# Edge messages on one core: the buckets' one-hot rows are made on ScalarE instead of VectorE

## The chip, the cores and the metric

The kernel runs on one core of one Trainium2 chip. The metric is the device time of one execution of the whole program in microseconds (us); the kernel before was timed in three runs and its median counts. One further execution was taken by the hardware profiler, and every row of a profile below is from such an execution.

The core's engines are named as in the profile: PE is the matmul engine (PEld its weight loads), DVE is VectorE, ACT is ScalarE, POOL is GpSimd, and SP is SyncE, which issues most of the transfers. Each engine runs its own instructions in the order in which they were written, and they wait for each other by semaphores. ACT and DVE have no way round an instruction that waits: what is written behind it waits as well.

## The reference

One layer of message passing on a graph of N = 12,500 nodes with 64 values each and E = 800,000 edges with 16 values each:

```
m_in = concatenate([x[src], x[dst], e_attr], axis=-1)
msg  = silu(m_in @ w_msg)                 # one row of 64 for each edge
agg  = segment_sum(msg, dst, N)           # summed by the edge's target
out  = silu(concatenate([x, agg], axis=-1) @ w_upd)
```

The targets `dst` come in no order, so the kernel sorts the edges into buckets of targets before it sums them.

## The kernel before

**Buckets and chunks.** The nodes are cut into 128 buckets of 98. The edges are read in chunks of M = 8 tiles of 128 edges, 782 chunks in all. `seg_prep` computes for each edge, 18 chunks at once, the bucket `hi` of its target (`floor_ops`) and the target's place `lo` in the bucket. A chunk then goes through five steps, each a method of `Chunk`:

- `onehot` (L362) writes `hf`, a row of 128 for each edge, which is 1 at the edge's bucket and 0 elsewhere: one DVE comparison over 8 x 128 = 1024 elements a partition.
- `sums` (L368 to L371) adds these rows over the tiles of each half of the chunk: the first piece is copied on ACT, the other three are DVE additions, into `G`.
- `count` (L379 to L381) multiplies `hf` and `G` on PE, which leaves in `z` the place of each edge among the edges of its bucket; `ranks` (L386) takes it out on DVE.
- `expand` (L395 to L399) lays the edges' records into slots `X` on DVE; `move` (L407) brings them to their buckets' rows by 16 PE instructions with `hf` as weights, and ACT copies the result to `blk` (L409); `place` (L415, L416) advances the buckets' pointers on DVE.
- `scatter` (L420) writes `blk` to the buckets' places in a store in HBM, by an indirect transfer that POOL issues.

**Groups and batches.** Whole tiles of sorted edges are taken from the store in groups of up to 64 tiles (`fourth`, `middle` and `fifth` choose them with small DVE operations and two small PE products, L511 and L518, which use the same PSUM buffer as `move`). A group is worked on in batches of 8 tiles: `gather` (L574) fetches the sources' rows by eight indirect transfers of POOL; `onehot` of the batch (L579, L580) makes rows `q` for the targets within the bucket; `transpose` (L588 on PE, copied by ACT at L591 into `qt`); `product` (L597, PE); `message` (L603 on DVE, then SiLU at L604 on ACT); `parts` (L612, two DVE subtractions that split the message into bf16 parts); `reduce` (L623, PE) and `add` (L636 and L638, DVE). The first groups take single tiles and pairs of tiles of a bucket; later ones take four tiles of a bucket at a time, and only these have `parts`.

**A period.** The function `period` interleaves one step of each of several chunks and batches, and its text is the order of every engine's instructions. In one call there are: the chunk `h` that begins, the chunk `z` that is one period old, the chunk `p` that is two periods old and `s` that is three; and the batches `q`, `t` and `a` of ages 0, 1 and 2. So what `onehot` and `sums` make in one period is used by `count` in the next, by `move` in the one after, and the buffer of `hf`, of which there are three, is written again after that. In each period, after the message of batch `a`, DVE does `hf`, `parts`, `G`, `q`, `rank`, `X`, the sums and the pointers; ACT does SiLU, two copies of weights, `qt`, the first piece of `G`, a part of `q`, `blk`, and in one period of three the records (L257). There are 782 periods with a chunk; behind them come periods with batches alone and the updates of the nodes.

Of the kernel before, what the change touches and what calls it, by code (L numbers as in the profile page):

```python
# [6 lines left out]
AF = mybir.ActivationFunctionType  # L7
OP = mybir.AluOpType
# [6 lines left out]
P = 128  # L15
NBK = 128
BK = 98
# [5 lines left out]
M = 8  # L23
# [20 lines left out]
def mpnn_kernel(tc, x, e_attr, src, dst, w_msg, w_upd, out):  # L44
    nc = tc.nc
# [21 lines left out]
    with es:  # L67
# [21 lines left out]
        iof = cp.tile([P, P], F32, name="iof")  # L89
# [22 lines left out]
        ioB = cb[:, 0:P]  # L112
# [107 lines left out]
        T1, GAP = NT - NT % M, -NT % M  # L220
# [11 lines left out]
        def seg_load(load, n):  # L232
            di = sg.tile([P, SEG], I32, name="sdi")
            si = sg.tile([P, SEG], I32, name="ssi")
            load(di[:, :n], dst_v)
            load(si[:, :n], src_v)
            return di, si

        def seg_prep(di, si, n, t0=0):
            hi = sg.tile([P, SEG], F32, name="shi")  # L240
            lo = sg.tile([P, SEG], F32, name="slo")
            floor_ops(hi[:, :n], lo[:, :n], di[:, :n], HI_SC, HI_OFF)
            nc.vector.scalar_tensor_tensor(out=lo[:, :n], in0=hi[:, :n], scalar=-float(BK), in1=di[:, :n], op0=OP.mult, op1=OP.add)
            k = max(0, T1 - t0)
            if k < n and GAP:

                nc.vector.memset(hi[:, k:T1 + GAP - t0], float(2 * P))
            return hi, lo, si

        def ea_load(load, n):  # L250
            ea = eap.tile([P, EAT, DE], F32, name="ea")
            load(ea[:, :n, :], ea_v)
            return ea

        def records(ea, si, lo, n):
            rec = eap.tile([P, EAT, R], F32, name="rec")
            nc.scalar.activation(rec[:, :n, 0:DE], ea[:, :n, :], AF.Copy)  # L257
            nc.vector.scalar_tensor_tensor(out=rec[:, :n, DE], in0=lo, scalar=1.0 / 256, in1=si, op0=OP.mult, op1=OP.add)
            return rec
# [10 lines left out]
        def prep_seg(i):  # L270
            if i < len(segs) and i not in ready:
                load_seg(i)
                ready[i] = seg_prep(*loaded[i], segs[i][1], segs[i][0])
# [80 lines left out]
        class Chunk:  # L354
# [4 lines left out]

            def onehot(c):  # L360
                c.hf = hp.tile([P, M, NBK], F32, name="hf")
                nc.vector.tensor_tensor(out=c.hf, in0=ioB[:, None, :].to_broadcast([P, M, NBK]), in1=c.hi[:, :, None].to_broadcast([P, M, NBK]), op=OP.is_equal)  # L362

            def sums(c):

# [277 lines left out]
        def period(chunk=None, batch=None, ptr_new=None):  # L643

            h, z, p, s = chunk, pipe["h"], pipe["z"], pipe["p"]
            q, t, a = batch, pipe["q"], pipe["t"]
            forms = [g for g in work["forming"] if not g.ready()]
            pipe.update(h=h, z=z, p=p, q=q, t=t)
            if z:
                z.count()  # L650
            if a:
                a.message()
            if t:
                t.transpose(0)
            if h:
                h.onehot()
            if t:
                t.weights()
                t.transpose(1)
            if q:  # L660
                q.gather(0, BT // 2)
            if s:
                s.scatter()
            if q:
                q.gather(BT // 2, BT)
            if a:
                a.parts()
            if h:
                h.sums()
            if q:  # L670
                q.onehot()
            if z:
                z.ranks()
            for g in forms:
                g.fourth()
            if z:
                z.expand()
            if p:
                p.move()
            if a:  # L680
                a.reduce()
                a.add()
            if p:
                p.place(ptr_new)
            for g in forms:
                g.middle()
                g.fifth()
            if t:
                t.product()
            return a  # L690
# [141 lines left out]
        while pipe["p"]:  # L832
            period(None, take())
# [11 lines left out]
        for k in range(0, NCH, 512):  # L845
            n = min(512, NCH - k)
# [124 lines left out]
        with tc.If(more > 0):  # L971
# [4 lines left out]
            with tc.If(nover > 0):  # L976
# [12 lines left out]
                for k in range(0, NCH, P):  # L989
                    n = min(P, NCH - k)  # L990
# [12 lines left out]
                with tc.For_i(0, nover, 1):  # L1003

                    nc.vector.tensor_reduce(out=f1[:, 3:4], in_=fl, axis=AX.X, op=OP.min)
                    nc.vector.scalar_tensor_tensor(out=fl, in0=fl, scalar=f1[:, 3:4], in1=fl, op0=OP.not_equal, op1=OP.mult)
                    nc.vector.tensor_scalar(out=f1[:, 2:3], in0=f1[:, 3:4], scalar1=BIG, scalar2=None, op0=OP.add)

                    w0 = cp.tile([1, 2], F32, name="w0")
                    nc.vector.tensor_scalar(out=w0[:, 0:1], in0=f1[:, 2:3], scalar1=float(M), scalar2=float(NT - M), op0=OP.mult, op1=OP.min)  # L1010
                    nc.vector.scalar_tensor_tensor(out=w0[:, 1:2], in0=f1[:, 2:3], scalar=float(M), in1=w0[:, 0:1], op0=OP.mult, op1=OP.subtract)
                    nc.vector.tensor_copy(fi[:, 2:3], w0[:, 0:1])
                    bps = pp.tile([P, 512], F32, name="bps", tag="pl")
                    nc.tensor.matmul(bps[:, 0:1], oner, w0[:, 1:2], start=True, stop=True)
                    skip = cp.tile([P, 1], F32, name="skip")
                    nc.vector.tensor_copy(skip, bps[:, 0:1])
                    tv = nc.values_load(fi[0:1, 2:3], engines=(ENG.SP,), min_val=0, max_val=NT - M, skip_runtime_bounds_check_because="the start of a chunk")
                    window = lambda buf, src: nc.sync.dma_start(buf, src[:, ds(tv, M)])
                    hi, lo, si = seg_prep(*seg_load(window, M), M, -NT)
                    rec = records(ea_load(window, M), si[:, :M], lo[:, :M], M)  # L1020
                    off = cp.tile([P, M], F32, name="off")
                    nc.vector.tensor_scalar(out=off, in0=iof[:, 0:M], scalar1=skip, scalar2=float(2 * P), op0=OP.is_lt, op1=OP.mult)
                    nc.vector.tensor_tensor(out=hi[:, :M], in0=hi[:, :M], in1=off, op=OP.add)
                    c = Chunk(hi[:, :M], rec[:, :M, :])
                    c.onehot()
                    c.sums()
                    c.count()
                    c.ranks()

                    c.expand()  # L1030
                    c.move()
                    left = cp.tile([NBK, 3], F32, name="left")
                    nc.vector.tensor_scalar(out=left[:, 1:2], in0=c.blk[:, 1:2], scalar1=0.0, scalar2=None, op0=OP.is_gt)
                    nc.vector.tensor_tensor(out=left[:, 0:1], in0=c.blk[:, 0:1], in1=left[:, 1:2], op=OP.mult)
                    nc.vector.memset(rs, 0.0)
# [39 lines left out]
```

## Time and profile before

| | |
|---|---|
| median of 3 runs | 11522.06 us (11520.64 to 11545.6) |
| the profiled execution, its own time | 11522.43 us |
| its span, from the first instruction to the last | 11520.6 us |
| mean granted clock of PE | 0.817 |
| first and last `hf` (L362) | 13.9 and 10592.5 us |

In the rows that follow, a row of a group gives line, engine, operation, what is written and read, shapes and count; behind the first bar the busy time in us and the mean duration of one in ns; behind the second the idle time of the engine just before these instructions, and what ended it. A row of the timeline gives the start and the duration in us, then engine, line and operation, and in square brackets the idle time before it. A releaser that is called "remote" or "another core or an unknown queue" is a semaphore update for which the profile finds no instruction that ended at that moment. On one core that is no other core.

### The profile page before, as it was taken

How to read it: one execution, taken by the hardware profiler on the slowest of the kernel's cores; microseconds unless marked ns; L12 is line 12 of the kernel's file. 1: busy time of each engine (PE TensorE's matmuls, PEld its weight loads, DVE VectorE, ACT ScalarE, POOL GpSimd, SP SyncE). 2: the span in 40 equal slices, each digit the busy share in tenths (PEclk: the TensorE clock that was granted, in tenths of full speed). 3: DMA queues.
4: the chain of work that ended last, by engine and by line, in shares of the span. 5: the costliest groups of instructions: out<-in, count | busy, mean ns of one | idle time of the engine just before them, and what ended most of it. 6: DMA issues, size and time to landing. Idle time of an engine off the chain costs nothing. (4 is left out here: it accounts for less than half of the span.)

```text
span 11520.6 us, 142616 instructions
## 1 busy us (share of the span) xinstructions
PE 8812.3 (76%) x43298; PEld 6708.3 (58%) x44060; DVE 8786.3 (76%) x18300; ACT 2487.4 (22%) x5785; POOL 6874.6 (60%) x7129
## 2 busy tenths in 40 slices
PE   7777777777777777777777777777777777777566
PEld 4555555555555555655655555565655565555466
DVE  8777777888888888878888888887888888887322
ACT  2111112222222222222222222222222222222111
POOL 2455556666666666666666666666666666666555
PEclk9888888888888888788888888888888888888555
DMA  2111111111111111111111111111111111111212
GB/s 64 39 43 46 41 44 49 44 47 46 44 47 44 48 43 47 47 44 47 44 47 44 46 47 44 47 44 47 47 43 47 45 46 47 43 46 41 44 36 39
DMA packets 661675, 521.39 MB, mean 45 GB/s; under 512 B 472583, under 2 KB 520135, under 8 KB 660903
## 3 DMA queue, kind: packets, MB, share of 16 engines
q0 software_dynamic: 252672, 378.89, 12.3%
q1 hardware_dynamic: 405527, 132.58, 5.2%
q8 instruction: 359, 5.88, 0.2%
q14 instruction: 413, 3.38, 0.1%
q10 hardware_dynamic: 2704, 0.66, 0.0%
HBM read 330.05 MB, written 181.46 MB: 44 GB/s over the span
## 5 line engine op out<-in xcount | busy, mean ns | idle before, releaser
L574 POOL DMA_INDIRECT g<-A_d,sidx x6322 | 6077.2, 961 | 3146.3 <-issue 1669.5
L407 PE MATMUL pl<-X,hf 128*128 128x427 f32 (+3 forms) x12512 | 3946.6, 463 | 637.9 <-issue 463.4
L407 PEld LDWEIGHTS pl<-X,hf 128*128 128x128 f32 x12512 | 2461.8, 203 | 1966.5 <-issue 1238.1
L399 DVE TENSOR_TENSOR X<-cb,rec 128x850 f32<-128x850 f32 (+3 forms) x3128 | 2379.7, 823 | 26.8
L597 PE MATMUL pre<-w,qt 114*128 114x64 f32 x10496 | 1725.2, 333 | 458.1 <-ACT qt L591 385.0
L597 PEld LDWEIGHTS pre<-w,qt 114*128 114x128 f32 x10496 | 1653.0, 247 | 507.1 <-ACT qt L591 421.3
L604 ACT ACTIVATE msg<-msg 128x512 f32<-128x512 f32 (+1 forms) x818 | 503.3, 615 | 5688.6 <-DVE msg L603 4660.0
L603 DVE TENSOR_TENSOR msg<-pre,g 128x512 f32<-128x512 f32 (+1 forms) x818 | 550.8, 673 | 1431.6 <-remote 1041.7
L420 POOL DMA_INDIRECT st<-blk,ptrs x781 | 779.2, 998 | 1389.4 <-ACT blk L409 1099.8
L588 PE MATMUL tq<-ident,q 128*114 128x128 f32 x6322 | 1109.2, 330 | 148.5 <-issue 83.6
L588 PEld LDWEIGHTS tq<-ident,q 128*114 128x114 f32 x6322 | 988.1, 170 | 347.9 <-issue 219.5
L623 PE MATMUL ag<-msg,q 128*98 128x192 bf16 x5248 | 650.1, 268 | 581.8 <-ACT q L580 197.5
L591 ACT ACTIVATE qt<-tq 114x1024 f32<-114x1024 f32 (+1 forms) x818 | 804.9, 984 | 1283.0 <-remote 867.2
L386 DVE TENSOR_REDUCE rank<-z 128x8 f32<-128x1024 f32 x782 | 950.3, 1215 | 96.4 <-remote 69.3
L612 DVE TENSOR_TENSOR msg<-msg 128x512 f32<-128x512 f32 x1312 | 906.5, 691 | 75.5 <-issue 26.6
L623 PEld LDWEIGHTS <-q 128*98 128x98 bf16 x5248 | 542.8, 135 | 707.1 <-issue 565.0
L362 DVE TENSOR_TENSOR hf<-cb,shi 128x1024 f32<-128x1024 f32 x782 | 949.9, 1215 | 0.0
L579 DVE TENSOR_TENSOR q<-cb,lo 128x784 f32<-128x784 f32 (+1 forms) x818 | 768.4, 939 | 0.0
L409 ACT ACTIVATE blk<-pl 128x427 f32<-128x427 f32 x782 | 407.9, 522 | 1469.7 <-PE pl L407 386.2
L380 PE MATMUL z<-G,onesb 128*128 128x384 bf16 x1564 | 636.3, 407 | 115.6 <-issue 86.8
L636 DVE TENSOR_REDUCE sum<-ag 98x128 f32<-98x384 f32 x656 | 361.4, 551 | 287.2 <-remote 142.5
L379 PE MATMUL z<-hf,w 128*128 128x512 bf16 x802 | 391.5, 488 | 46.4 <-issue 27.8
(141 smaller groups left out, 6154.7 us busy)
## 6 DMA issues: line engine op xcount, KB each, us to landing
g<-A_d,sidx POOLq DMA_INDIRECT x6322
ea<-in_e_attr SPq DMA_DIRECT2D x260, 192.0 KB
rt<-st SPq DMA_DIRECT2D x1312, 34.0 KB
st<-blk,ptrs POOLq DMA_INDIRECT x781
rt<-st SPq DMA_DIRECT2D x434, 8.5 KB
nodes<-in_x SPq DMA_DIRECT2D x62, 98.0 KB
rt<-st SPq DMA_DIRECT2D x320, 17.0 KB
A_d<-nodes SPq DMA_DIRECT2D x32, 98.0 KB
```

Source lines behind the costliest of these rows:

```text
L362: nc.vector.tensor_tensor(out=c.hf, in0=ioB[:, None, :].to_broadcast([P, M, NBK]), in1=c.hi[:, :, None].to_broadcast([P, M, NBK]), op=OP.i ...
L386: nc.vector.tensor_reduce(out=c.rank, in_=c.z, axis=AX.X, op=OP.max)
L399: nc.vector.tensor_tensor(out=c.x[:, k:k + 2, 2:2 + n * R].rearrange("p k (s c) -> p k s c", c=R), in0=hit[:, k:k + 2, 0:n, None].to_broad ...
L407: nc.tensor.matmul(pl[:, 0:w], c.hf[:, k, :], c.x[:, k, 0:w], start=(k == M - 1), stop=(k == 0))
L420: i = nc.gpsimd.indirect_dma_start(out=st, out_offset=bass.IndirectOffsetOnAxis(ap=c.ptr, axis=0), in_=c.blk[:, 2:XR], in_offset=None)
L574: nc.gpsimd.indirect_dma_start(out=t.g[:, i, :], out_offset=None, in_=A_d, in_offset=bass.IndirectOffsetOnAxis(ap=t.grp.sidx[:, k:k + 1], ...
L579: nc.vector.tensor_tensor(out=t.q[:, 0:n, 0:BK], in0=ioB[:, None, 0:BK].to_broadcast([P, n, BK]), in1=t.grp.lo[:, i0:i0 + n, None].to_broa ...
L588: nc.tensor.transpose(t.tq[0:KQ, j * P:(j + 1) * P], t.q[:, j, :], ident)
L591: nc.scalar.activation(t.qt[:, 0:w], t.tq[0:KQ, 0:w], AF.Copy)
L597: nc.tensor.matmul(t.pre[:, i * D:(i + 1) * D], t.qt[:, i * P:(i + 1) * P], w, start=True, stop=True)
L612: nc.vector.tensor_tensor(out=t.msg[:, k + 1, :], in0=t.msg[:, k, :], in1=up[:, k, :, 1], op=OP.subtract)
L623: nc.tensor.matmul(t.ag[0:BK, u * w:(u + 1) * w].rearrange("p (k d) -> p k d", d=D), q[:, i, :], m[:, :, i * D:(i + 1) * D], start=(k == 0 ...
```

## The change

ACT makes `hf`. Its row for a tile is the square of the distance between each of the numbers 0 to 127 and the tile's bucket, which is 0 at the bucket and at least 1 elsewhere; one less that, not below zero, is the one-hot row. For this `seg_prep` stores the bucket with the other sign, which changes constants and one operand's sign and no number of instructions. ACT's square takes the bucket as a bias, one number a partition, so it is one instruction for each of the 8 tiles; the last step is one instruction over all 1024 elements. In `period`, `onehot` of the chunk is written behind the batch's `weights` and `transpose`, and `sums` behind the batch's `onehot` and the chunk's `ranks`.

```
 def onehot(c):
     c.hf = hp.tile([P, M, NBK], F32, name="hf")
-    nc.vector.tensor_tensor(out=c.hf, in0=ioB[:, None, :].to_broadcast([P, M, NBK]), in1=c.hi[:, :, None].to_broadcast([P, M, NBK]), op=OP.is_equal)
+    for k in range(M):
+        nc.scalar.activation(c.hf[:, k, :], iof, AF.Square, bias=c.hi[:, k:k + 1])
+    nc.scalar.activation(c.hf, c.hf, AF.Relu, bias=ones, scale=-1.0)
```

```
 if t:
     t.transpose(0)
-if h:
-    h.onehot()
 if t:
     t.weights()
     t.transpose(1)
+if h:
+    h.onehot()
...
 if a:
     a.parts()
-if h:
-    h.sums()
 if q:
     q.onehot()
 if z:
     z.ranks()
+if h:
+    h.sums()
 for g in forms:
     g.fourth()
```

```
-floor_ops(hi[:, :n], lo[:, :n], di[:, :n], HI_SC, HI_OFF)
-nc.vector.scalar_tensor_tensor(out=lo[:, :n], in0=hi[:, :n], scalar=-float(BK), in1=di[:, :n], op0=OP.mult, op1=OP.add)
+floor_ops(hi[:, :n], lo[:, :n], di[:, :n], -HI_SC, -HI_OFF)
+nc.vector.scalar_tensor_tensor(out=lo[:, :n], in0=hi[:, :n], scalar=float(BK), in1=di[:, :n], op0=OP.mult, op1=OP.add)
...
-    nc.vector.memset(hi[:, k:T1 + GAP - t0], float(2 * P))
+    nc.vector.memset(hi[:, k:T1 + GAP - t0], -float(2 * P))
```

One more line with the changed sign, `off`, lies in a branch for chunks that did not fit their slots.

After the change ACT's order in a period is: SiLU, weights, `qt`, eight squares, the last step of `hf`, a part of `q`, the first piece of `G`, `blk`, and the records in one period of three. DVE's is: message, `parts`, `q`, `rank`, the three additions of `G`, `X`, sums, pointers. PE, POOL and SP have the same instructions in the same order as before.

More of the change, by code (lines that the diff above doesn't have):

```diff
@@ L654, in period @@
                 t.transpose(0)
-            if h:
-                h.onehot()
             if t:
@@ L659, in period @@
                 t.transpose(1)
+            if h:
+                h.onehot()
             if q:
@@ L667, in period @@
                 a.parts()
-            if h:
-                h.sums()
             if q:
@@ L673, in period @@
                 z.ranks()
+            if h:
+                h.sums()
             for g in forms:
@@ L1022, in mpnn_kernel @@
                     nc.vector.tensor_scalar(out=off, in0=iof[:, 0:M], scalar1=skip, scalar2=float(2 * P), op0=OP.is_lt, op1=OP.mult)
-                    nc.vector.tensor_tensor(out=hi[:, :M], in0=hi[:, :M], in1=off, op=OP.add)
+                    nc.vector.tensor_tensor(out=hi[:, :M], in0=hi[:, :M], in1=off, op=OP.subtract)
                     c = Chunk(hi[:, :M], rec[:, :M, :])
```

## The prediction

> **What bounds the kernel now.** I read the page's head first, then the idle times of DVE and ACT by line, then one stretch of the timeline.
>
> ```profile
> span 11520.6 us, 142616 instructions
> PE 8812.3 (76%) x43298; PEld 6708.3 (58%) x44060; DVE 8786.3 (76%) x18300; ACT 2487.4 (22%) x5785; POOL 6874.6 (60%) x7129
> ```
>
> PE and DVE are equally busy, so shares name no bound; ACT has room. The groups between 2000 and 10500 us, where 612 messages were made, say who waits (DVE's and ACT's groups, then the list of waits of the same stretch):
>
> ```profile
> L362 DVE TENSOR_TENSOR hf<-cb,shi 128x1024 f32<-128x1024 f32 x612 | 743.4, 1215 | 0.0
> L603 DVE TENSOR_TENSOR msg<-pre,g 128x512 f32<-128x512 f32 x612 | 423.4, 692 | 1050.2 <-remote 724.3 <-DMA st<-blk,ptrs 62.4 <-DMA g<-A_d,sidx 58.9
> L636 DVE TENSOR_REDUCE sum<-ag 98x128 f32<-98x384 f32 x612 | 337.0, 551 | 250.2 <-remote 122.9 <-PE tq L588 60.4 <-PE pre L597 34.7
> L591 ACT ACTIVATE qt<-tq 114x1024 f32<-114x1024 f32 x611 | 619.2, 1013 | 1154.2 <-remote 802.6 <-issue 135.4 <-PE ag L623 107.3
> ...
> DVE msg L603 <- remote: 724.3, 172, 8.9
> ACT qt L591 <- remote: 802.6, 135, 11.3
> ```
>
> A period there takes 8500/612 = 13.9 us. DVE's idle time sits almost wholly at two places that wait for PE, the message and the sums: (1050.2 + 250.2)/612 = 2.1 us a period. So DVE's own chain takes 11.8 us, and PE's lateness the rest. At L603 the long waits are few: 172 of the 612, 4.2 us each; the other 440 periods have (1050.2 - 724.3)/440 = 0.7 us or less each, and there DVE comes near to setting the pace. The third wait matters for what follows: `qt` on ACT waits for PE's transposes, 1154.2/611 = 1.9 us a period, in 135 long ones 5.9 us each. Nothing on DVE waits for that now. One period of the timeline:
>
> ```profile
> 5000.96 0.69 DVE L603 TENSOR_TENSOR msg<-pre,g 128x512 f32<-128x512 f32 x1 [0.15 <-issue]
> 5001.57 1.22 DVE L362 TENSOR_TENSOR hf<-cb,shi 128x1024 f32<-128x1024 f32 x1
> 5001.74 0.63 ACT L604 ACTIVATE msg<-msg 128x512 f32<-128x512 f32 x1 [2.06 <-DVE msg L603]
> 5002.70 1.41 DVE L612 TENSOR_TENSOR msg<-msg 128x512 f32<-128x512 f32 x2
> 5002.82 1.00 ACT L591 ACTIVATE qt<-tq 114x1024 f32<-114x1024 f32 x1
> 5003.73 0.40 ACT L368 ACTIVATE G<-hf 128x256 bf16<-128x256 f32 x1
> 5004.02 0.42 DVE L370 TENSOR_TENSOR G<-hf 128x256 bf16<-128x256 f32 x1
> 5004.03 0.30 ACT L580 ACTIVATE q<-rt 128x128 f32<-128x128 f32 x1
> 5005.15 0.97 DVE L579 TENSOR_TENSOR q<-cb,lo 128x784 f32<-128x784 f32 x1
> 5006.03 1.22 DVE L386 TENSOR_REDUCE rank<-z 128x8 f32<-128x1024 f32 x1
> 5007.28 0.17 DVE L395 TENSOR_TENSOR X<-rank,limc 128x8 f32<-128x8 f32 x1
> 5011.90 0.22 DVE L416 SCALAR_TENSOR_TENSOR ptrs<-blk,LOST,ptrs 128x1 int32<-128x1 f32 x1
> 5019.93 0.69 DVE L603 TENSOR_TENSOR msg<-pre,g 128x512 f32<-128x512 f32 x1 [6.45 <-remote]
> ```
>
> With T for the start of the message (5000.96): `hf` covers the SiLU; `parts` begins at T+1.74, the first addition of `G` at T+3.06, `X` at T+6.32, and DVE is done at T+11.2. The next message then waits 6.45 us: one of PE's late spells.
>
> **The change part by part.** *Removed:* 782 comparisons of 1.215 us on DVE, 950 us, all of them in DVE's chain. If DVE's busy time were what counts, that would be the gain; it is not, since the chain now passes through ACT.
>
> *`parts` loses its cover.* SiLU ends at 5002.37, T+1.41. Behind the message, which gives way at T+0.61, DVE has now nothing before `parts`, which starts at some T+1.5, so that of the 1.13 us from 5001.57 to 5002.70 some 0.9 comes back as idle time. `parts` then takes 1.32 us (5002.70 to 5004.02), `q` 0.88, `rank` 1.25 (the starts of the next rows): DVE reaches `sums` at T+4.95.
>
> *`hf` on ACT.* It is queued behind SiLU, weights and `qt`, and `qt` gives way where L368 started, T+2.77. No square and no operation with a bias of one number a partition is in the trace. The nearest row is a copy of the same 128x128 numbers, L580: alone it takes 0.30 us, and next to another copy the two lie 0.20 apart:
>
> ```profile
> 5218.56 0.30 ACT L580 ACTIVATE q<-rt 128x128 f32<-128x128 f32 x1
> 5218.76 0.52 ACT L409 ACTIVATE blk<-pl 128x427 f32<-128x427 f32 x1
> ...
> L183 ACT ACT_TABLE_LOAD x1 | 1.3, 1283 | 14.5 <-DMA wu<-in_w_upd 14.5
> L604 ACT ACT_TABLE_LOAD x1 | 1.3, 1283 | 0.0
> ```
>
> Eight squares take 8 x 0.20 = 1.6 us if they overlap like copies, and 8 x 0.30 = 2.4 if they do not; nothing here tells which, so I take 2.0, and 0.1 for the last to end. The last step has as many elements a partition as `qt`, 1.0 us, with 0.1 for its wait on the squares. `hf` is then ready at T+2.77+2.1+1.1 = T+5.97, and DVE, there since T+4.95, idles 1.1 us. `G` takes 1.13 us (5004.02 to 5005.15), so `X` starts at T+7.2 in place of T+6.32. **DVE's chain grows by 0.9 us a period although an operation of 1.2 us has left it** (0.45 with overlapping squares, 1.25 without).
>
> The Trainium skill, in ScalarE: Activation LUTs, section What ACT_TABLE_LOAD costs, says that a pointer operand of one number a partition adds about 93 ns to an activation and that neighbours overlap by about 93 ns. The trace agrees with the second half (0.30 alone, 0.20 apart); no run here shows the first. By it the squares would lie 0.29 apart, and my sum would be an estimated 0.3 us a period higher.
>
> *`sums` moved.* `G` and `hf` are read by `count` of the next period, which had to wait for `rank` at T+6.28 and now waits for `G` at T+7.2. PE gets there after `reduce` and `product`; in periods that DVE paces, PE has until T+11.2 and more, so I cost this at nothing. Where PE is late it costs up to 0.9.
>
> *Behind the squares on ACT* stand a part of `q`, `blk` and the records. `q` is needed a period later. `blk` can be copied from T+6.5 on instead of from the end of `move`; who waits are DVE's pointers, at T+10.7 or later, POOL's scatter (POOL is busy 60%), and the small products of a group, which share `move`'s buffer:
>
> ```profile
> L511 PE MATMUL ps<-wl,tri 128*128 128x1 f32 x152 | 35.0, 300 | 198.2 <-ACT blk L409 125.2 <-DVE wl L482 36.8 <-DVE wl L478 29.9
> ```
>
> Up to 2 us more for each of the 152 is 300 us of PE's time, which its idle quarter covers: nothing, up to +300 where PE is late. *Constants and signs in `seg_prep`* change no count: nothing.
>
> *The early stage.* Up to 1800 us there are 149 chunks with smaller batches and no `parts`:
>
> ```profile
> L362 DVE TENSOR_TENSOR hf<-cb,shi x149: 1202/1215/1219, 13.9 to 1799.6; 128x1024 f32<-128x1024 f32 x149
> ...
> L603 DVE TENSOR_TENSOR msg<-pre,g x112: 557/558/692, 282.0 to 1749.7; 128x384 f32<-128x384 f32 x105, 128x512 f32<-128x512 f32 x7
> ...
>   remote: 90.2, 40
> ...
> 1112.81 0.56 DVE L603 TENSOR_TENSOR msg<-pre,g 128x384 f32<-128x384 f32 x1
> 1114.59 0.42 ACT L368 ACTIVATE G<-hf 128x256 bf16<-128x256 f32 x1
> 1117.47 0.22 DVE L487 TENSOR_SCALAR mat<-iof,wl 128x12 f32<-128x12 f32 x1
> ```
>
> Here ACT is free for squares at T+1.78, `hf` is ready at T+1.78+3.2 = T+4.98, and DVE gets past `G` at T+6.1 instead of T+4.66: 1.5 us a period, of which the long waits at L603, 40 of 112, absorb their share.
>
> *The wait for late transposes becomes DVE's.* `hf` stands on ACT behind `qt`. So the 1.9 us a period that `qt` waits for PE, which cost nothing, now push back `hf`, `G`, `X` and the next message, since DVE stands at `G` already.
>
> **Sum.** DVE is asked to wait 0.9 + 1.9 = 2.8 us a period more. What can take this in are the waits that it has, 2.1 us: a spell in which PE is late is met once, and DVE that has waited at `G` finds the next message's product done. I take this exchange as complete, since both waits come of the same late semaphores; then 0.7 us a period are left: 633 chunks x 0.7 = 440 us. Early: 149 x 0.64 x 1.5 = 143. Behind 10592 us nothing changes. Together +580 us on the profiled run's own 11522.4, which is the median's equal: **12100 us**. With 0.45 or 1.25 in place of 0.9 (and 1.1 or 1.9 early) the same sum gives 11790 and 12370.
>
> **The rivals.** *A: the waits add up.* The exchange is not complete: PE's next `count` waits for the `G` that came late, so PE is late again. For it speaks that PE, busy 76%, has little to catch up with. If half of the 2.1 us is left standing, the price is 633 x 1.05 = 665 us more, 12770; if all, 13430. Against it: a PE that starts later does not work longer, and its idle quarter is there for it.
>
> *B: PE sets the pace.* If PE's rate does not depend on DVE, the period stays at 13.9 us and all that DVE waits for more is waited for less elsewhere. For it speaks that PE's share is the same early and late while DVE's is not:
>
> ```profile
> 1100.00:1700.00 600.00, 468.17 (x2428) 347.49 (x2475) 451.89 (x1099) 112.12 (x252) 315.78 (x329) 0.88 0.17 43
> 6000.00:8000.00 2000.00, 1560.15 (x7620) 1179.79 (x7765) 1626.94 (x3292) 450.82 (x1059) 1253.80 (x1295) 0.83 0.17 46
> ```
>
> PE 0.78 and 0.78, DVE 0.75 and 0.81. Against it: the asked 2.8 us exceed the 2.1 there are, and 440 of 612 periods have no long wait. Time: 11520 to 11700, the early stage's part at most.
>
> *C: faster.* PE's late spells may come of DVE's running ahead: after a stretch that DVE paces, PE has less slack. A slower DVE leaves PE time, and the spells shrink. If a share a of the lateness goes for good, the change is 633 x (0.9 - 2.1a) + 149 x 1.5, below zero from a = 0.6 on; at a = 0.75 it is -200 us, 11320. Against it: nothing in the trace shows that the spells follow DVE.
>
> *D: not what it says.* If square and SiLU could not stay loaded together, each period would pay two table loads of 1.283 us, 782 x 2.57 = 2000 us on ACT's chain. The kernel before loads twice in all (the two rows above), and the changed program has two loads as well, so this hardly counts.
>
> **How the numbers follow.** Forecast 0.50, A 0.24, B 0.13, C 0.12, D 0.01. A measurement of this kernel tells 0.2% (23 us) from no change. Faster: C and a little of B, 0.13; same: 0.05 of B; slower: the rest, 0.82. The likeliest is 12100 (its own range 11790 to 12370). The range leaves out C and the upper part of A: 11520 to 12800.
>
> **What would show it.** Right: DVE busy falls by some 950 us and the idle time at L612 rises from next to nothing to 0.7 us or more each; the first addition of `G` gets an idle time of 1.1 us where `qt` is in time and of several us where it is late, 3 us a period in the mean, released by ACT's last step of `hf`; `X` follows the message by 7.2 us in the undisturbed periods; ACT is busy some 2400 us more; the waits at L603 shrink. Squares 0.20 or 0.30 apart show in the timeline. A shows as idle time at L603 hardly less than the 1050 us of now; B as an unchanged period, C as less idle time at `qt` and L603 together. Wrong would be a forecast in which the wait at `G` is short because ACT is ahead of DVE, or one in which `blk`, late on ACT, holds up PE's small products and POOL's scatter.

## The result, and the profile after

| | before | after |
|---|---|---|
| median beside each other (4 runs each) | 11525.28 us (11520.64 to 11545.6) | 11707.11 us (11685.04 to 11725.39) |
| profiled execution, its own time | 11522.43 us | 11685.04 us |
| mean granted clock of PE | 0.817 | 0.825 |

The change makes the kernel slower: 1.0153 times the time before, interval 1.0132 to 1.0175. That is +182 us by the medians and +163 us by the two profiled executions. The sign is the one forecast, the size is a third of the +580 us of the forecast.

First the head of the page of the changed kernel.

```profile
span 11683.2 us, 146831 instructions
PE 8923.2 (76%) x43298; PEld 6658.1 (57%) x44060; DVE 7929.2 (68%) x17518; ACT 5147.8 (44%) x12823; POOL 7021.9 (60%) x7129
```

DVE has lost 857 us of busy time and ACT has gained 2660. Where the 163 us lie is read from the first and the last `rank`, one to a chunk. The rows give the count, the shortest, median and longest one in ns, and from when to when they started: for the 149 early chunks and for all 782, of the kernel before and then of the changed one.

```profile
L386 DVE TENSOR_REDUCE rank<-z x149: 1210/1215/1225, 29.5 to 1815.5; 128x8 f32<-128x1024 f32 x149
L386 DVE TENSOR_REDUCE rank<-z x782: 1208/1215/1226, 29.5 to 10613.2; 128x8 f32<-128x1024 f32 x196
```

```profile
L390 DVE TENSOR_REDUCE rank<-z x149: 1202/1215/1226, 31.9 to 1942.8; 128x8 f32<-128x1024 f32 x149
L390 DVE TENSOR_REDUCE rank<-z x782: 1202/1215/1226, 31.9 to 10776.6; 128x8 f32<-128x1024 f32 x196
```

The early stage ends 1942.8 - 1815.5 = 127 us later. The 633 late periods took 10613.2 - 1815.5 = 8797.7 us before and 10776.6 - 1942.8 = 8833.8 after: +36 us, or 13.90 and 13.96 us a period. Behind the last chunk the difference is -1 us. So the early stage came out near its forecast of 143, and the late one far below its 440.

Now who waits in the late stage. These are the groups of the changed kernel between 2000 and 10500 us (609 messages), the counterparts of the rows shown of before.

```profile
L607 DVE TENSOR_TENSOR msg<-pre,g 128x512 f32<-128x512 f32 x609 | 421.2, 692 | 510.9 <-remote 335.2 <-PE z L385 39.7 <-PE tq L592 35.0
L616 DVE TENSOR_TENSOR msg<-msg 128x512 f32<-128x512 f32 x1218 | 847.7, 696 | 444.3 <-issue 218.4 <-ACT msg L608 205.2
L374 DVE TENSOR_TENSOR G<-hf 128x256 bf16<-128x256 f32 x610 | 259.6, 426 | 999.3 <-issue 597.2 <-ACT hf L366 402.1
L640 DVE TENSOR_REDUCE sum<-ag 98x128 f32<-98x384 f32 x609 | 334.0, 548 | 136.5 <-remote 107.5 <-PE tq L592 22.4 <-issue 4.3
...
L365 ACT ACTIVATE hf<-iof,shi 128x128 f32<-128x128 f32 x4880 | 1484.1, 389 | 0.0
L366 ACT ACTIVATE hf<-hf,ones 128x1024 f32<-128x1024 f32 x610 | 700.1, 1148 | 19.8
L595 ACT ACTIVATE qt<-tq 114x1024 f32<-114x1024 f32 x609 | 613.3, 1007 | 144.0 <-remote 58.3 <-PE tq L592 53.6 <-PE ag L627 30.1
```

Per period DVE now idles 444.3/609 = 0.73 us at `parts` and 999.3/610 = 1.64 at `G`, which is new. At the message and the sums it idles (510.9 + 136.5)/609 = 1.06 us, where it was 2.12. And `qt` on ACT, which waited 1.9 us a period for PE, waits 144.0/609 = 0.24. That wait did not move to DVE: it has all but gone.

One undisturbed period of the changed kernel, DVE and ACT in order of start; T is 5007.32.

```profile
5007.32 0.69 DVE L607 TENSOR_TENSOR msg<-pre,g 128x512 f32<-128x512 f32 x1
5008.05 0.63 ACT L608 ACTIVATE msg<-msg 128x512 f32<-128x512 f32 x1 [5.86 <-issue]
5008.71 1.42 DVE L616 TENSOR_TENSOR msg<-msg 128x512 f32<-128x512 f32 x2 [0.69 <-issue]
5009.01 1.00 ACT L595 ACTIVATE qt<-tq 114x1024 f32<-114x1024 f32 x1
5009.91 2.43 ACT L365 ACTIVATE hf<-iof,shi 128x128 f32<-128x128 f32 x8
5010.93 1.22 DVE L390 TENSOR_REDUCE rank<-z 128x8 f32<-128x1024 f32 x1
5012.38 1.15 ACT L366 ACTIVATE hf<-hf,ones 128x1024 f32<-128x1024 f32 x1
5013.56 0.42 DVE L374 TENSOR_TENSOR G<-hf 128x256 bf16<-128x256 f32 x1 [1.42 <-issue]
5014.69 0.17 DVE L399 TENSOR_TENSOR X<-rank,limc 128x8 f32<-128x8 f32 x1
```

`X` starts at T+7.37, against T+6.32 before: the chain through ACT is 1.05 us longer, as the forecast had it (0.9, between 0.45 and 1.25). So the chain was foreseen and the period was not: 1.05 us more in DVE's chain lengthened the late period by 0.06 us.

### The profile page after: what moved, and what is told of

It reads as the page before. It is cut to its first block, busy times and chain, and to the rows that moved or that the text cites. A ratio compares the mean times of both kernels' runs of the same rounds, so it can differ in the third digit from the quotient of the medians.

```text
span 11683.2 us, 146831 instructions
## 1 busy us (share of the span) xinstructions
PE 8923.2 (76%) x43298; PEld 6658.1 (57%) x44060; DVE 7929.2 (68%) x17518; ACT 5147.8 (44%) x12823; POOL 7021.9 (60%) x7129
## 5 line engine op out<-in xcount | busy, mean ns | idle before, releaser
L578 POOL DMA_INDIRECT g<-A_d,sidx x6322 | 6219.8, 984 | 3206.8 <-issue 1782.8
L411 PE MATMUL pl<-X,hf 128*128 128x427 f32 (+3 forms) x12512 | 3989.5, 468 | 527.0 <-issue 296.0
L365 ACT ACTIVATE hf<-iof,shi 128x128 f32<-128x128 f32 x6256 | 1902.5, 389 | 0.0
L601 PE MATMUL pre<-w,qt 114*128 114x64 f32 x10496 | 1625.9, 320 | 65.1 <-issue 47.7
L601 PEld LDWEIGHTS pre<-w,qt 114*128 114x128 f32 x10496 | 1567.8, 236 | 71.4 <-issue 46.5
L374 DVE TENSOR_TENSOR G<-hf 128x256 bf16<-128x256 f32 x782 | 332.7, 425 | 1473.5 <-issue 778.8
L592 PE MATMUL tq<-ident,q 128*114 128x128 f32 x6322 | 1159.6, 339 | 209.0 <-issue 100.4
L592 PEld LDWEIGHTS tq<-ident,q 128*114 128x114 f32 x6322 | 1020.7, 175 | 404.8 <-issue 253.7
L627 PE MATMUL ag<-msg,q 128*98 128x192 bf16 x5248 | 614.8, 262 | 567.4 <-DVE msg L616 350.2
L366 ACT ACTIVATE hf<-hf,ones 128x1024 f32<-128x1024 f32 x782 | 897.5, 1148 | 25.4
```

Source lines behind the costliest of these rows:

```text
L365: nc.scalar.activation(c.hf[:, k, :], iof, AF.Square, bias=c.hi[:, k:k + 1])
L366: nc.scalar.activation(c.hf, c.hf, AF.Relu, bias=ones, scale=-1.0)
L411: nc.tensor.matmul(pl[:, 0:w], c.hf[:, k, :], c.x[:, k, 0:w], start=(k == M - 1), stop=(k == 0))
L578: nc.gpsimd.indirect_dma_start(out=t.g[:, i, :], out_offset=None, in_=A_d, in_offset=bass.IndirectOffsetOnAxis(ap=t.grp.sidx[:, k:k + 1], ...
L592: nc.tensor.transpose(t.tq[0:KQ, j * P:(j + 1) * P], t.q[:, j, :], ident)
L601: nc.tensor.matmul(t.pre[:, i * D:(i + 1) * D], t.qt[:, i * P:(i + 1) * P], w, start=True, stop=True)
```

## The experiments

Two readings were to be told apart. By the forecast's, DVE's chain and PE's lateness together make the period, and what is added to the chain beyond the waits that it has is paid. By the other, the late periods have a pace of their own, and the waits at the message, the sums and `qt` are what is left of the period when a chain is shorter than that. The kernels ran in four sets, each set on one chip with the kernel before beside it. On the chips of three sets the kernel before takes 11430 to 11550 us, as on the chip of the result; on the chip of one set it takes 9582 us. They are called the 11,500 chips and the 9,582 chip below.

### DVE's chain made longer, on an 11,500 chip

On this chip the kernel before took 11537.25 us.

```
     c.hf = hp.tile([P, M, NBK], F32, name="hf")
+    for _ in range(2):
-    nc.vector.tensor_tensor(out=c.hf, ..., op=OP.is_equal)
+        nc.vector.tensor_tensor(out=c.hf, ..., op=OP.is_equal)
```

> The kernel before, with DVE's comparison for hf made twice in a row (same result): 1.2 us more in DVE's chain in each of the 782 periods and nothing else. Theory P (PE sets the pace of the late periods, about 13.9 us each, as long as DVE's own chain is shorter; here 11.8 + 1.2 = 13.0): the late 633 periods stay within 0.1 us of 13.9, the 149 early ones pay, total +100 to +250 us, 11620 to 11780. Theory F (the forecast: DVE's chain sets the pace in most periods, and what saved the change is particular to ACT): 0.7 x 1.2 x 782 = +650 us or more, above 12150.

Measured: 11492.7 us, ratio 0.9962 (0.9948 to 0.9976). 782 x 1.215 = 950 us were put into the chain that ends each period, and the kernel became 45 us faster. Neither expected range holds that: P had +100 to +250 us, F +650 or more. Its ranks:

```profile
L387 DVE TENSOR_REDUCE rank<-z x149: 1205/1215/1225, 29.4 to 1912.6; 128x8 f32<-128x1024 f32 x149
L387 DVE TENSOR_REDUCE rank<-z x782: 1205/1215/1225, 29.4 to 10588.8; 128x8 f32<-128x1024 f32 x196
```

The early stage is 1912.6 - 1815.5 = 97 us longer (the row of before is from another chip of the kind; `order_only` below, on this chip and with a chain as long, has its 149th rank at 1816.1 us and late periods of 13.90), of 149 x 1.215 = 181 us put in. The late periods take (10588.8 - 1912.6)/633 = 13.71 us, so none of their 1.215 us is paid.

The same with a third comparison, `range(3)`:

> As the one before, with the comparison three times: 2.4 us more, DVE's chain 14.2 us. P: now past the knee: late periods at 14.2 plus what is left of the waits, +0.3 to +1.3 us each (+190 to +820), early ones +250 to +360, 11970 to 12700, and the second 1.2 us cost two to five times as much as the first. F: both extra comparisons cost the same, above 12800.

Measured: 11963.88 us, ratio 1.0364 (1.0347 to 1.0382), 6 us below P's range. Its ranks:

```profile
L387 DVE TENSOR_REDUCE rank<-z x149: 1211/1215/1226, 30.4 to 2044.7; 128x8 f32<-128x1024 f32 x149
L387 DVE TENSOR_REDUCE rank<-z x782: 1209/1214/1226, 30.4 to 11054.4; 128x8 f32<-128x1024 f32 x196
```

Its messages in the groups between 2000 and 10000 us:

```profile
L604 DVE TENSOR_TENSOR msg<-pre,g 128x512 f32<-128x512 f32 (+1 forms) x562 | 388.3, 691 | 104.9 <-issue 27.4 <-remote 21.7 <-PE pl L408 11.8
```

The late period is (11054.4 - 2044.7)/633 = 14.23 us, and the wait at the message has shrunk to 104.9/562 = 0.19 us: now DVE's chain of 11.7 + 2.43 = 14.1 us sets the pace. Between the second comparison and the third lies a knee. Below it the late period does not follow the chain.

ACT has the same instructions in both kernels as before the change. Its `qt` in the groups between 2000 and 10000 us, with the comparison made twice and then three times:

```profile
L592 ACT ACTIVATE qt<-tq 114x1024 f32<-114x1024 f32 x583 | 587.3, 1007 | 255.8 <-remote 115.1 <-PE ag L624 90.8 <-PE pl L408 24.9
L592 ACT ACTIVATE qt<-tq 114x1024 f32<-114x1024 f32 x562 | 566.1, 1007 | 36.2 <-PE tq L589 25.5 <-PE ag L624 5.8 <-issue 2.0
```

It waits 255.8/583 = 0.44 us and 36.2/562 = 0.06 us a period, where it waited 1.9. ACT comes to `qt` behind SiLU, and SiLU waits for DVE's message. So a longer chain on DVE alone takes the wait at `qt` away.

### The order alone, and the chain made shorter

Two kernels take the change apart on the same chip. `order_only` has the change's places for `onehot` and `sums` with `hf` still made on DVE:

```
-if h:
-    h.onehot()
 if t:
     t.weights()
     t.transpose(1)
+if h:
+    h.onehot()
...
-if h:
-    h.sums()
 if q:
     q.onehot()
 if z:
     z.ranks()
+if h:
+    h.sums()
```

> The kernel before with the change's order alone: hf stays on DVE, sums stand behind the batch's one-hot and the chunk's rank. P and F: DVE's chain has the same length, within 30 us of before. If the earlier rank (which frees z for PE) is what saved the change 400 us, this alone gains 100 us or more; if the later G holds PE up, it loses as much.

Measured: 11521.74 us, ratio 0.9983 (0.9973 to 0.9993). The new order, with `hf` still on DVE, costs nothing.

`act_first` makes `hf` on ACT as the change does, but one step ahead: the squares stand at the end of ACT's list, `G` right behind the message.

```
+if h:
+    h.onehot()
...
 if a:
     a.message()
+if h:
+    h.sums()
...
-if h:
-    h.onehot()
...
-if h:
-    h.sums()
```

> The changed kernel, with ACT's one-hot rows written at the head of the period, ahead of the message, and sums right behind the message as before the change: ACT has the squares done in the idle time ahead of SiLU, DVE waits for nothing of it, and DVE's chain is 1.1 us shorter than before the change, 10.7 us. P: the late periods stay at 13.7 to 13.9 (PE), only the early ones gain, up to 149 x 1.1 = 160 us: 11300 to 11530. F: 0.7 x 1.1 x 782 = -600 us, about 10900. Third theory (the late spells of PE come of DVE running ahead, so that a faster DVE makes them worse): 11530 or more.

Measured: 11541.76 us, ratio 1.0005 (0.9995 to 1.0014). By its number this lies where the third theory had it (11530 or more); of the two others, P missed it by 12 us and F by far. Here `hf` is nearly always ready when `G` asks for it (between 2000 and 10000 us `G` waits 154.7/574 = 0.27 us a period), and the comparison has left DVE's chain, 1.215 us a period. Its ranks:

```profile
L390 DVE TENSOR_REDUCE rank<-z x149: 1208/1215/1226, 35.1 to 1823.3; 128x8 f32<-128x1024 f32 x149
L390 DVE TENSOR_REDUCE rank<-z x782: 1206/1214/1226, 35.1 to 10626.7; 128x8 f32<-128x1024 f32 x196
```

Its message and `qt` in the groups between 2000 and 10000 us:

```profile
L607 DVE TENSOR_TENSOR msg<-pre,g 128x512 f32<-128x512 f32 x574 | 396.9, 692 | 1243.6 <-remote 685.1 <-PE pre L601 160.5 <-PE pl L411 146.5
L595 ACT ACTIVATE qt<-tq 114x1024 f32<-114x1024 f32 x575 | 581.6, 1011 | 1155.6 <-remote 638.6 <-PE ag L627 350.5 <-PE tq L592 110.7
```

The late period is (10626.7 - 1823.3)/633 = 13.91 us, that of before, and the early stage gained nothing either, where P had up to 160 us. What DVE no longer does, it waits: 1243.6/574 = 2.17 us at the message alone. `qt` waits 2.0 us again, as before the change, although ACT makes all the squares here. So the wait at `qt` is no fixed property of PE's transposes; it is long where DVE's message, and ACT behind it, comes early.

### PE's work made less and more, and the change on the 9,582 chip

If the pace is PE's, less work on PE should shorten it. `product_bf16` makes the products of the late batches from the upper halves of the words of `qt` and of the weights, so as bf16; the lower halves are left out.

```
-nc.tensor.matmul(t.pre[...], t.qt[...], w, start=True, stop=True)
+qh = t.qt.bitcast(BF16).rearrange("k (p two) -> k p two", two=2)[:, i * P:(i + 1) * P, 1]
+wh = t.w.bitcast(BF16).rearrange("k u (d two) -> k u d two", two=2)[:, u, :, 1]
+nc.tensor.matmul(t.pre[...], qh, wh, start=True, stop=True)
```

> The kernel before with PE's product in bf16 in the late batches (the upper halves of qt and w; the messages lose their lower bits): 8 PE instructions in place of 16, and shorter ones. PE's records give the product 2.6 us a period before, and 8 bf16 instructions of reduce, which are wider, 1.0: 1.6 us of PE's time less. P (PE sets the late pace): late periods fall from 13.9 by 1.0 to 1.6 us, down to DVE's chain at the least, -630 to -1000 us, 10530 to 10900. F (DVE's chain sets it in seven periods of ten): at most a quarter of that, above 11270.

`product_twice` makes each of these products twice into the same place, `for _ in range(2)`:

> The kernel before with every product of the late batches made twice (same result): 2.6 us more of PE's time a period by the records. P: late periods +1.9 to +2.6 us, +1200 to +1650 us in all, 12700 to 13200. F: the periods that DVE paces hide most of it, below 12100.

`product_bf16_after` is the changed kernel with the edit of `product_bf16`:

> The changed kernel with the product in bf16 as in product_bf16. With PE out of the way the longer chain of the change must show: P: the late periods are DVE's, 12.9 to 13.2 us, so this is 400 to 700 us slower than product_bf16 (early stage +125 of it), and no less than 300 us faster than the change. If the change's chain is not longer at all: equal to product_bf16 but for the early stage.

`dve_twice_late` repeats the comparison only in periods whose groups take four tiles of a bucket, `for _ in range(2 if state["u"] == QU else 1)`:

> The kernel before with the comparison for hf made twice in the late stage alone. If the late gain of dve_twice (13.90 to 13.71 us a period) is real and apart from its early loss of 97 us: 11380 to 11440, faster than before by 0.7 to 1.2%. If gain and loss belong together (time moved from one stage to the other): 11490 to 11540.

These four ran on the 9,582 chip: the kernel before took 9581.94 us. The expectations had the first chip's numbers in mind and can be read against this one only as differences. Measured: `product_bf16` 9581.31 (ratio 1.000, 0.9991 to 1.001), `product_twice` 9788.07 (1.0221, 1.0204 to 1.0238), `product_bf16_after` 10454.82 (1.0911, 1.0893 to 1.0929), `dve_twice_late` 10391.66 (1.0845, 1.0827 to 1.0863). `product_bf16` gained nothing and `product_twice` cost 206 us, as F had it and not P. `product_bf16_after` lies 873 us above `product_bf16`, where 400 to 700 were expected, and `dve_twice_late` 810 us above the kernel before, where it was to be faster or equal: both missed.

The head of the page of `product_bf16` shows another machine, although its program is that of before but for the products:

```profile
PE 7267.4 (76%) x38349; PEld 5247.9 (55%) x38812; DVE 8766.4 (92%) x18300; ACT 2442.3 (25%) x5785; POOL 6879.1 (72%) x7129
```

Its message and `qt` in the groups between 2000 and 8500 us:

```profile
L608 DVE TENSOR_TENSOR msg<-pre,g 128x512 f32<-128x512 f32 x555 | 384.0, 692 | 76.4 <-issue 32.3 <-DMA g<-A_d,sidx 26.2 <-DMA st<-blk,ptrs 0.8
L591 ACT ACTIVATE qt<-tq 114x1024 f32<-114x1024 f32 x555 | 557.0, 1004 | 0.0
```

DVE is 92% busy. It waits 76.4/555 = 0.14 us a period at the message, `qt` never waits, and in its list of waits between 2000 and 10000 us none is "remote". Here DVE's chain does set the pace, and the change is paid in full. The ranks of `product_bf16`, then of `product_bf16_after`:

```profile
L386 DVE TENSOR_REDUCE rank<-z x149: 1207/1215/1226, 29.6 to 1471.8; 128x8 f32<-128x1024 f32 x149
L386 DVE TENSOR_REDUCE rank<-z x782: 1207/1215/1226, 29.6 to 8883.8; 128x8 f32<-128x1024 f32 x196
```

```profile
L390 DVE TENSOR_REDUCE rank<-z x149: 1203/1215/1226, 31.9 to 1688.8; 128x8 f32<-128x1024 f32 x149
L390 DVE TENSOR_REDUCE rank<-z x782: 1203/1215/1226, 31.9 to 9762.2; 128x8 f32<-128x1024 f32 x196
```

And `G` of the latter in the groups between 2000 and 8500 us:

```profile
L374 DVE TENSOR_TENSOR G<-hf 128x256 bf16<-128x256 f32 x509 | 216.4, 425 | 720.6 <-ACT hf L366 720.6
```

Early +217 us, 1.46 a period. Late (8883.8 - 1471.8)/633 = 11.71 us becomes (9762.2 - 1688.8)/633 = 12.75, +1.04 us a period or 661 us. These are the prediction's two terms of the chain (1.5 and 0.9) with nothing to take them in. The wait at `G`, 720.6/509 = 1.42 us, is that of the undisturbed period in the timeline above.

### The same on 11,500 chips

To compare like with like, four kernels ran together on such a chip, where the kernel before took 11432.6 us: the changed kernel, `act_first`, and the two with PE's products changed.

> The changed kernel, on whichever chip comes. Two kinds of chip have been seen: on one (L) PE's semaphores come late in spells and before takes 11540 us, on the other (N) they never do and before takes 9580. Theory P-L (PE's late spells are the chip's, and they alone hid the change's longer chain): on L again 11690 to 11730; on N the whole chain is paid, 633 x 1.05 + 149 x 1.45 = +880 us, 10400 to 10500, 9% slower. Theory O (the change itself thins out the spells, by its order or by ACT's work): on N there are no spells to thin out, so it says the same there, but it wants a gain on L that a mere delay on DVE does not give, and dve_twice had it already.

> The version with ACT's one-hot rows at the head of the period. On L: as before it, 11520 to 11560, since PE sets the pace. On N: DVE's chain is 1.1 us shorter, 10.6 us; next bound is POOL, eight gathers of 1.25 us from start to start and a scatter of 1.3, 11.3 us a period in the late stage and 8.8 in the early one: 633 x 0.35 + 149 x 0.9 = -350 us, 9150 to 9350. If nothing but DVE bounds N: 782 x 1.1 = -860, 8720.

> The kernel before with the late products in bf16, 1.6 us less of PE a period. On L: if the spells are PE's pace under load, 630 to 1000 us faster, 10530 to 10900; if the spells have nothing to do with how much PE does, within 150 us of before. On N: as measured there, equal to before.

> The kernel before with the late products made twice. On L: if PE's load sets the pace, +1200 to +1650 us, 12700 to 13200; if the spells are something that stops PE for a time of its own, whatever its load, no more than the +200 us that it cost on N. On N: 9790 as measured.

Measured: `change_again` 11610.52 us (ratio 1.0148, 1.013 to 1.0167), `act_first_again` 11433.85 (0.9999, 0.9989 to 1.0008), `product_bf16_again` 11337.42 (0.992, 0.9903 to 0.9936), `product_twice_again` 11727.68 (1.026, 1.0243 to 1.0277). The change and `act_first` repeat in their ratios. `product_bf16_again` stayed within its 150 us; `product_twice_again` cost 295 us, more than the 200 of one theory and far less than the 1200 of the other. The head of the page of `product_bf16_again`:

```profile
PE 7771.9 (69%) x38812; PEld 5443.6 (48%) x38812; DVE 8793.6 (78%) x18300; ACT 2473.5 (22%) x5785; POOL 6917.9 (61%) x7129
```

The largest of the "remote" lines in its list of waits between 2000 and 10000 us (sum in us, count, the longest one):

```profile
ACT qt L591 <- remote: 835.9, 104, 11.2
ACT blk L409 <- remote: 465.6, 99, 9.1
DVE msg L608 <- remote: 390.2, 109, 8.2
DVE sum L641 <- remote: 217.9, 110, 6.7
DVE rank L386 <- remote: 130.5, 52, 5.3
```

The same program takes 9581 us on one chip and 11337 on another. On the second, every reader of PE's results has some 50 to 110 waits of up to 5 to 11 us which end when the profile sees no instruction end; on the first there are none. PE's busy time fell by 8812.3 - 7771.9 = 1040 us (the first figure is that of before on the chip of the result) and the kernel gained 95. The products made twice cost 295. So PE's load counts for something, but far less than it would if PE's work were the pace.

The last four kernels took more of PE's work away, on a chip where the kernel before took 11549.54 us. `move`, PE's largest group, uses the upper halves of `hf` and `X` (the lower halves of the records are left out, so other sources are gathered than before):

```
-nc.tensor.matmul(pl[:, 0:w], c.hf[:, k, :], c.x[:, k, 0:w], start=(k == M - 1), stop=(k == 0))
+hb = c.hf.bitcast(BF16).rearrange("p m (b two) -> p m b two", two=2)[:, k, :, 1]
+xb = c.x.bitcast(BF16).rearrange("p m (b two) -> p m b two", two=2)[:, k, 0:w, 1]
+nc.tensor.matmul(pl[:, 0:w], hb, xb, start=(k == M - 1), stop=(k == 0))
```

in the kernel before:

> The kernel before with move in bf16 (the upper halves of hf and X: the records lose lower bits, so sources and messages come out changed, while counts, places and all control stay exact): 8 PE instructions in place of 16 and about half of PE's longest work. On a chip of kind L: if the spells come of PE's heavy work, the late periods fall towards DVE's chain, 13.8 to 12.5 or less, -800 us or more; if they are independent of PE's load, as product_bf16_again says, -100 to -250 us. On N: within 0.5% of before.

in the changed kernel:

> The changed kernel with move in bf16. If move_bf16 frees the kernel of the spells (or on N): the whole longer chain is paid, 850 to 900 us over move_bf16. If the spells stay: 1 to 3% over move_bf16, as the change stands to before on L.

in `act_first`:

> ACT's one-hot rows at the head of the period, with move in bf16. Spells gone or N: DVE's chain is 1.1 us shorter and POOL bounds next, 350 us below move_bf16. Spells stay: equal to move_bf16 within 0.3%.

and in the kernel before together with the edit of `product_bf16`:

> Move and the late products in bf16 in the kernel before: 16 PE instructions fewer a period, nearly 4 us of PE's time. On L, spells that follow PE's load: 1000 us or more below before. Spells independent of it: 200 to 400 us below before. On N: within 0.5% of before.

Measured: `move_bf16` 11546.78 us (ratio 1.000, 0.999 to 1.0009), `move_bf16_after` 11722.87 (1.0146, 1.0127 to 1.0165), `move_bf16_first` 11464.47 (0.9927, 0.991 to 0.9943), `both_bf16` 11459.6 (0.9927, 0.991 to 0.9944). `move_bf16` and `both_bf16` gained 3 and 90 us, less than either theory expected; `move_bf16_first` lies 0.7% below `move_bf16`, where 0.3% at most was expected. The heads of the pages of `move_bf16` and `both_bf16`:

```profile
PE 7175.7 (62%) x37396; PEld 5573.9 (48%) x37804; DVE 8775.9 (76%) x18300; ACT 2466.2 (21%) x5785; POOL 6878.6 (60%) x7129
```

```profile
PE 5754.9 (50%) x32167; PEld 4107.3 (36%) x32556; DVE 8789.8 (77%) x18300; ACT 2461.7 (22%) x5785; POOL 6895.4 (60%) x7129
```

PE's busy time falls from 8812 (again on the chip of the result) to 5755 us, by 3057, and the kernel gains 90 us. The change costs 1.5% with `move` halved, as it does without. So the pace of the late stage on these chips is neither DVE's chain nor the sum of PE's work.

By the waits in the lists, results of PE are announced late there. PE itself stops as well. In the late spell that ends the prediction's timeline of the kernel before, its instructions of `move` come nearly one at a time:

```profile
5014.27 0.41 PE L407 MATMUL pl<-X,hf 128*128 128x291 f32 x1 [0.95 <-issue]
5016.37 0.41 PE L407 MATMUL pl<-X,hf 128*128 128x291 f32 x1 [1.69 <-issue]
5017.76 0.41 PE L407 MATMUL pl<-X,hf 128*128 128x291 f32 x1 [0.99 <-issue]
5019.86 2.13 PE L407 MATMUL pl<-X,hf 128*128 128x291 f32 x5 [1.69 <-issue]
```

"issue" is a wait for nothing that the profile shows. Between 2000 and 10500 us of the kernel before those at `move` are (sum in us, count, the longest one):

```profile
PE pl L407 <- issue: 392.3, 434, 2.8
```

In the lists of `product_bf16` and `product_twice` on the 9,582 chip, between 2000 and 8500 us, there is no such line. These stops are 392.3/612 = 0.6 us a period, a part of the 2.2 us that lie between 11.71 and 13.90. What stops PE, and whether this is what makes its results late, no run shows.

### What the runs say together

Late periods in us, each worked out from ranks as above; on the 11,500 chips, before and the change are from the chip of the result, the other three from one more. The chain of DVE is the period on the 9,582 chip where it was measured (the kernel before stands there as `product_bf16`, equal to it in time, the change as `product_bf16_after`); the first and the last are estimates, 11.71 less one comparison and plus two.

| kernel | DVE's chain | 9,582 chip | 11,500 chips |
|---|---|---|---|
| `act_first` | 10.5 (11.71 - 1.215) | | 13.91 |
| before | 11.7 | 11.71 | 13.90 |
| the change | 12.75 | 12.75 | 13.96 |
| comparison twice (late) | 13.0 | 12.97 | 13.71 |
| comparison three times | 14.1 (11.71 + 2.43) | | 14.23 |

On the 11,500 chips the period stays between 13.7 and 14.0 while the chain goes from 10.5 to 13.0, and rises when the chain passes it.

No version here is shown to beat the kernel before on both kinds of chip with the same result. The doubled comparison gains 0.4% on an 11,500 chip, but in the late periods alone it costs 8.5% on the 9,582 chip. `act_first` equals the kernel before on 11,500 chips and was not run on the other, where its shorter chain should pay; that is argued, not shown. The changed kernel was run on the 9,582 chip only with its products in bf16.

## Why the prediction was right or wrong

*The chain through ACT: right.* `parts` idles 0.73 us instead of 0.9. Eight squares end 2.43 us after the first began; one takes 0.389, so they lie (2.43 - 0.39)/7 = 0.29 us apart. With the last to end they take 2.43 instead of 2.1, the last step 1.15 instead of 1.1, and `X` comes 1.05 us later instead of 0.9. (By the prediction's own times `hf` is ready 5.97 - 4.95 = 1.02 us after DVE asks, and `X` starts at 5.97 + 1.13 = T+7.1, so the 0.9 should have been 0.8, some 60 us less in the forecast.) On the 9,582 chip the late period grew by 1.04 us.

The Trainium skill's rule on a pointer operand (ScalarE: Activation LUTs, section What ACT_TABLE_LOAD costs) holds here: a square takes 389 ns where the copy of the same shape takes 299 ns before, 90 ns less, against the page's 93. The two differ in their function too, and no run parts that from the operand.

*The early stage: right.* Forecast 143 us, measured 127. Asked were 1.5 us a period (the 9,582 chip shows 1.46), and 127/(149 x 1.46) = 0.58 of it was paid, where 0.64 was taken. The doubled comparison paid 97 of 181, 0.54.

*Moves without a price: right.* `order_only` shows that the new order by itself, with `hf` on DVE, costs nothing. For the small products and `blk` the forecast had nothing, and up to +300 us where PE is late; nothing in the time answers to that.

*"The wait for late transposes becomes DVE's": wrong, and this is the step that failed.* The prediction took the 1.9 us that ACT waited at `qt` for a fixed demand, put it on top of the 0.9, set 2.1 us of DVE's own waits against 2.8, and paid the 0.7 left: 440 us. But `qt` waits 0.24 us after the change, 2.0 in `act_first`. Such a wait is what is left of the period when the engine's own chain is shorter. When DVE's chain grew, the message came later, ACT behind it came to `qt` later and found the transposes done: with more comparisons on DVE and nothing changed on ACT, `qt` waits 0.44 and 0.06. DVE's idle time is 3.43 us a period now (0.73, 1.64 and 1.06) and was 2.12, 1.31 more; 1.215 of that is the comparison that is gone, and the 0.1 left is the late period's 0.06 as well as these rows can tell. The old waits took in nearly all of the 1.05 us that the chain grew by, and 1.06 us of them are still there.

*Rival B was the mechanism.* It was given 0.13 and the range 11520 to 11700; the median of the change lies 7 us above it, the profiled execution inside. Its reason in the prediction, that PE's rate does not depend on DVE, is half right: the rate does not depend on DVE's chain below some 13.7 us, but it is not PE's work that makes it. What was held against B was the sum of 2.8 us, itself the faulty step. The prediction's formula for C would give +128 us with half the lateness gone, near the result too; one run of the change could not have told them apart. What does is that the period stands still from a chain of 10.5 us to one of 13.0, and that the chain is paid in full where nothing comes late. A trace of C is left, since the late periods of the doubled comparison are 0.2 us shorter than those before, and `act_first`, with a shorter chain, is no faster; why is not shown.

*A and D fell.* The wait at the message did not stay: 1050.2 us became 510.9. ACT loads its tables twice, as before:

```profile
L183 ACT ACT_TABLE_LOAD x1 | 1.3, 1283 | 14.8 <-DMA wu<-in_w_upd 14.8
L608 ACT ACT_TABLE_LOAD x1 | 1.3, 1283 | 0.0
```

*The signs named beforehand.* The wait at `parts`, the 7.2 us from message to `X` and the smaller wait at the message came as named. The 3 us at `G` did not (1.64), and that was the sign of the failed step; the sign named for B, an unchanged period, did: 13.90 and 13.96. The sign named for C, less idle time at `qt` and at the message together, came too; it tells nothing for C, since the kernel with three comparisons shows it as well and is slower. DVE's busy time fell by 857 us where 950 was named, and ACT's rose by 2660 where 2400 was.

## What to carry to other kernels

Idle time behind a late producer is not yet a demand: it may be what is left of a period that something else sets, and then it shrinks by itself when the waiting engine comes later. Before such a wait is moved on paper to another engine, find the pace: put a known operation into the chain once and twice and take one out; a period that does not move has another owner, and the knee shows how far the chain may grow. And price a change also for a chip on which that owner is absent: here the same 1.05 us cost 0.06 a period on one kind of chip and 1.04 on another.

## What was not expected of the hardware

The kernel before takes 9582 us on one chip and 11433 to 11550 on the others met. The two kinds differ in waits that end with no instruction's end: none on the first, hundreds on the second, up to 11 us each. Only one chip of the faster kind was met, in one set of runs, so it is not shown whether the difference is the chip's or that of its state at the time.

More work made the kernel faster: 950 us of repeated comparisons on DVE gave 0.9962 of the time.

With PE's work taken away its granted clock fell and the time did not follow, on three executions of 11447 to 11538 us (the kernel before, `move_bf16`, `both_bf16`; span and mean clock):

```profile
core 0: 11520.6 us, clock 0.817
```

```profile
core 0: 11537.6 us, clock 0.688
```

```profile
core 0: 11447.0 us, clock 0.664
```

The Trainium skill (TensorE: Matmul & The Clock Gate, section Part 1: The HAM clock gate (the "warmup" mystery)) says that the idle state is the throttled one and that activity releases it. The direction agrees: less work, a lower clock.
